# Second MoE of a fused attention and two-MoE kernel: its first product by seven products of blocks, and its loops with two blocks of tokens outermost

## The chip, the cores and the metric

The kernel runs on 1 core of a Trainium2 chip. Times are device microseconds (us) of that core for one execution; the runs of the kernel before have a median of 1211.6 us (3 runs, 1210.45 to 1211.93).

## What is computed

```python
attn = memory_attention(q, k, v, phi)          # 4 batches, 8 heads, 576 tokens, 64 wide
x = tokens_by_heads(attn)                      # 2304 x 512
h = x @ moe_w_in                               # first MoE, 2048 hidden
x = maximum(0.01 * h, h) @ moe_w_out
p = probs / (probs.sum(-1) + 1e-9)             # second MoE, 4 experts, 1024 hidden
for e in range(4):
    out += p[:, e:e + 1] * (maximum(x @ w1[e], 0) @ w2[e])
```

All of it is float32. A matmul here takes rounded operands (`float32r`), so every factor is split into a rounded high part and a rounded remainder, and every product is three matmuls: low x high, high x low, high x high.

## The kernel before

One list of operations, `Plan`, holds every step with an engine, a planned duration, a due time, and the tiles it reads and writes. `Plan.issue` walks a planned clock and, on each engine, issues the ready operation with the earliest due time; an operation with `also=` may go to a second engine. What comes out is a fixed order per engine, and the chip follows it, each instruction waiting for its semaphores. PSUM is eight banks, taken and given back through `Banks`.

Attention and the first MoE come first (up to about 409 us), then the second MoE. In its loops before, the expert is outermost, then the six blocks of TB = 384 tokens, then the eight chunks of 128 hidden units: 4 x 6 x 8 = 192 steps (`moe2_step`). A step is 12 matmuls of 384 columns for the first product (line 746: 4 pieces of the 512 inputs, 3 matmuls each), the rectifier on ScalarE (line 874, from PSUM, rounding to `hh`), the remainder on VectorE (line 876, from PSUM, to `hl`), and 9 matmuls of 512 columns for the second product (lines 889 to 891: 3 tiles of 128 tokens, 3 matmuls each). After eight chunks the three sums leave PSUM (line 899 on ScalarE for the first expert, line 901 on VectorE for the others). Tokens are split into parts again for each expert (`x_part`, through `split`, lines 224 and 227); weights are fetched once, into `raw` tiles by SP's queue, and split by `piece32`: the high part on ScalarE (line 224), the remainder on GpSimd or VectorE (line 227).

Of the kernel before, what the change touches and what calls it, by code (L numbers as in the profile page):

```python
# [19 lines left out]
class Banks:  # L20


    def __init__(self, psum, n):
        self.psum, self.n, self.at, self.uses = psum, n, None, 0
# [5 lines left out]
class Plan:  # L30
# [38 lines left out]
    def take(self, free, bank):  # L69

        if bank.at is not None:
            return True
        if bank.n == 2:
            at = [i for i in range(0, self.BANKS, 2) if {i, i + 1} <= free]
        else:
            at = sorted(free, key=lambda i: (i ^ 1) in free)
        if not at:
            return False
        bank.at = at[0]
        free.difference_update(range(at[0], at[0] + bank.n))  # L80
        return True

    def issue(self):
# [14 lines left out]
        while issued < len(ops):  # L98
            now = events[0][0]
            while events and events[0][0] <= now:  # L100
                _, n, what = heappop(events)
                if what is not None:
                    if isinstance(what, Banks):
                        banks.update(range(what.at, what.at + what.n))
                    continue
                for e, queue in zip(ops[n][0], (ready, spare)):
                    heappush(queue[e], (ops[n][1], n))
# [37 lines left out]
def kernel(  # L145
# [19 lines left out]
    P = 128  # L165
# [22 lines left out]
    AHEAD = 10.0  # L188
    MARGIN = 7.0
# [5 lines left out]
    const = ctx.enter_context(tc.tile_pool(name="const", bufs=1))  # L195
    wa = ctx.enter_context(tc.tile_pool(name="wa", bufs=1))
    beside = tc.tile_pool(name="m1", bufs=1, side="right")
    m1 = beside.__enter__()
# [5 lines left out]
    pr = const.tile([P, NTILE, E], F32, name="pr")  # L204
    raws = [const.tile([P, 1024], F32, name=f"raw{i}") for i in range(RAWS)]
    f64s = [const.tile([P, 512], F32, name=f"f64{i}") for i in range(F64S)]
    hh = [const.tile([P, TB], F32R, name=f"hh{i}") for i in range(NH)]
    hl = [const.tile([P, TB], F32R, name=f"hl{i}") for i in range(NH)]
    acc_all = const.tile([P, B - 1, KD, S], F32, name="acc")
    acc1 = [acc_all[:, b] for b in range(B - 1)]  # L210
    ah = [m1.tile([P, NGB, S], F32R, name=f"ah{b}") for b in range(B)]
    al = [m1.tile([P, NGB, S], F32R, name=f"al{b}") for b in range(B)]
    vt = m1.tile([P, B, HG, M], F32, name="vt")
    yh = [m1.tile([P, NGB, 2 * P], F32R, name=f"yh{i}") for i in range(NY)]
    yl = [m1.tile([P, NGB, 2 * P], F32R, name=f"yl{i}") for i in range(NY)]
    gt = [m1.tile([P, HB], F32, name=f"gt{i}") for i in range(NH)]
# [80 lines left out]

    cuts = [0] + UNITS1 + [NC1]
    units1 = [range(a, z) for a, z in zip(cuts, cuts[1:])]
    units2 = [range(NC1 + e * NC2, NC1 + (e + 1) * NC2) for e in range(E)]  # L300
# [9 lines left out]
    for u, unit in enumerate(units2):  # L310
        for j in range(NB):
            for i, c in enumerate(unit):
                steps.append((2, u, j, 0, c, u * NB + j, i == 0, i == len(unit) - 1))
# [5 lines left out]
    for i in range(n1, len(steps), NC2):  # L319
        for kk in range(KD):  # L320
            behind.setdefault(max(n1, i - NC2 + 2 + kk), []).append(("x", steps[i][5], kk))
    t = 0.0
    when = []
    for i, st in enumerate(steps):
# [4 lines left out]
        t += 3.95 if st[0] == 2 else 2.22 * (1.6 if st[1] == 0 else 1.0)  # L329
# [4 lines left out]
    attp = tc.tile_pool(name="attp", bufs=1)  # L334
    ap = attp.__enter__()
    ident = ap.tile([P, P], F32, name="ident")
# [3 lines left out]
    spare = acc_all.rearrange("p b k s -> p (b k s)")  # L340
    sizes = [HG * NC * M, HG * NC * D, 2 * HG * NC * D]
    alt = [spare[:, sum(sizes[:i]):sum(sizes[:i + 1])] for i in range(3)]
    pl = [ap.tile([P, HG, NC, M], F32, name="pl"), alt[0].rearrange("p (h c m) -> p h c m", h=HG, c=NC)]
    ql = [ap.tile([P, HG, NC, D], F32, name="ql"), alt[1].rearrange("p (h c d) -> p h c d", h=HG, c=NC)]
    kv = [
        ap.tile([P, 2, HG, NC, D], F32, name="kv"),
        alt[2].rearrange("p (i h c d) -> p i h c d", i=2, h=HG, c=NC),
    ]
    eT = ap.tile([P, NC * P], F32, name="eT")
    qT = ap.tile([P, 2, S], F32, name="qT")  # L350
    kb = ap.tile([P, 2, 2, M], F32, name="kb")
    pt = ap.tile([P, NC, HG, M], F32, name="pt")
    qt = ap.tile([P, NC, HG, D], F32, name="qt")
    a = ap.tile([P, NC, P], F32, name="a")
    k2 = ap.tile([P, 2, 2, D], F32, name="k2")
    NR = S // M
    at = [ap.tile([P, NR, M], F32, name=f"at{i}") for i in range(2)]
    aT = ap.tile([P, S], F32, name="aT")
    small = {
        nm: [ap.tile([P, n], F32, name=f"{nm}{i}") for i in range(2)]  # L360
        for nm, n in (("nmx", 1), ("z", 1), ("rz", 1), ("mx", NR), ("sm", NR))
# [222 lines left out]

    late = {}

    def att_done():
        attp.__exit__(None, None, None)
        accb = ctx.enter_context(tc.tile_pool(name="accb", bufs=1))
        acc1.append(accb.tile([P, KD, S], F32, name="acc3"))  # L590
        late["wb"] = ctx.enter_context(tc.tile_pool(name="wb", bufs=1))

# [3 lines left out]
    plan.op("X", 0.0, 0.0, att_done, [], everything + ["attention"])  # L596
# [7 lines left out]
    NA, RING = {"w1": 3, "w2": 6}, {"w1": 5, "w2": 10}  # L604
    got = {}

    def tiles(kind, n):
        if (kind, n) not in got:
            at = n % RING[kind]
            pool = wa if at < NA[kind] else late["wb"]  # L610
            shape = [P, KD, 2 * P] if kind == "w1" else [P, DM]
            if kind == "w1" and n < NP1:
                nm = f"w1h{at}"
                got[kind, n] = (pool.tile(shape, F32, tag=nm, name=nm),)
            else:
                got[kind, n] = [
                    pool.tile(shape, F32R, tag=f"{kind}{x}{at}", name=f"{kind}{x}{at}") for x in "hl"
                ]
        return got[kind, n]

# [16 lines left out]
    def piece32(kind, n, sl, src, due, key, after):  # L637
        raw, rk = raw_piece(src, due, after)

        size = 256 * src.shape[1] if kind == "w1" else DM  # L640
        split(due, size, lambda: tiles(kind, n)[0][sl], lambda: tiles(kind, n)[1][sl], lambda: raw, [rk],
              [key + "h", key + "l"])
# [39 lines left out]
    def pieces_of(kind, n):  # L682

        if kind == "w1" and n < NP1:
# [3 lines left out]
        elif kind == "w1":  # L688
            e, p = divmod(n - NP1, NP2)
            w1 = moe2_w1[e][:, 2 * P * p:2 * P * (p + 1)].rearrange("(k p) f -> p k f", p=P)  # L690
            yield partial(piece32, kind, n, (every, every), w1)
        elif n < NC1:
            yield partial(piece64, kind, n, (every, every), moe_w_out[n * P:(n + 1) * P, :])
        else:
            e, c = divmod(n - NC1, NC2)
            yield partial(piece32, kind, n, (every, every), moe2_w2[e][c * P:(c + 1) * P, :])

    wanted = {}
    for t, op in when:
        if op[0] == "y":  # L700
            wanted.setdefault(("w1", ys[op[1]][2]), t)
        elif op[0] == "s":
            if steps[op[1]][0] == 2:
                wanted.setdefault(("w1", steps[op[1]][4] // 2), t - AHEAD)
            wanted.setdefault(("w2", steps[op[1]][4]), t)
    parts = sorted((t, key) for key, t in wanted.items())
# [17 lines left out]
    def w_keys(kind, n):  # L724
        at = n % RING[kind]
        return [f"{kind}.{at}.{i}{x}" for i in range(2) for x in "hl"]

    def load_part(kind, n):
        at = n % RING[kind]
        after = ["attention"] if at >= NA[kind] else []  # L730
# [6 lines left out]
    freed = {"w1": 0, "w2": 0}  # L737
# [40 lines left out]
    def moe1_step(t, n):  # L778
# [22 lines left out]
        for d in range(KD):  # L801
# [10 lines left out]
            if last:  # L812
                key = ("acc", b, s, d)

                def fn(e="DVE", d=d, po=po):
                    a_ = acc1[b][:, d, s * HB:(s + 1) * HB]
# [4 lines left out]
                if u == 0:  # L821
                    after = ["attention"] if b == B - 1 else ["alt"]
# [5 lines left out]
    acc2, x2, pos = [], [], []  # L828

    def second():  # L830

        beside.__exit__(None, None, None)
        m2 = ctx.enter_context(tc.tile_pool(name="m2", bufs=1, side="right", reuse_waits="tile"))
        x2.extend([m2.tile([P, KD, TB], F32R, name=f"x{x}{i}") for x in "hl"] for i in range(2))
        acc2.extend(m2.tile([P, TPB, DM], F32, name=f"acc2{j}") for j in range(NB))

    def x_part(t, n, kk):

        x, j = n % 2, n % NB
        t -= AHEAD + 2.0  # L840
        at_ = j * TB
        while at_ < (j + 1) * TB:
            b, o = divmod(at_, S)
            m = min((j + 1) * TB - at_, S - o)
            xs = slice(at_ - j * TB, at_ - j * TB + m)

            def part(i, xs=xs):
                return x2[x][i][:, kk, xs]

            def src(b=b, o=o, m=m):  # L850
                return acc1[b][:, kk, o:o + m]
            split(t, m, partial(part, 0), partial(part, 1), src,
                  [("acc", b, s, kk) for s in range(2)] + ["second"], [f"xh{x}{kk}", f"xl{x}{kk}"])
            at_ += m

    def moe2_step(t, n):
        _, u, j, _, c, m, first, last = steps[n]
        h, x = n % NH, m % 2
        ph = Banks(psum, 1)
        cs = slice((c % 2) * P, (c % 2 + 1) * P)  # L860
# [99 lines left out]
```

## Time and profile before

| what | before |
|---|---|
| median of 3 runs | 1211.6 us |
| profiled execution, its own time | 1211.6 us |
| its span, first to last instruction | 1209.8 us |
| TensorE busy in the span | 98% |
| VectorE, ScalarE, GpSimd busy | 37%, 33%, 12% |
| mean granted TensorE clock, share of full | 0.993 |
| DMA, mean over the span | 46 GB/s |

A matmul's record overlaps the next one's, so what one costs is read from start to start. "Idle before" an instruction is time in which its engine stood still, with the engine and line that ended the wait.

### The profile page before, as it was taken

To read this page: it belongs to the slowest core of one execution; us is meant where nothing else is said; L and a number is where in the kernel's file an instruction comes from. 1 tells how busy PE (TensorE), PEld (TensorE's weight loads), DVE (VectorE), ACT (ScalarE), POOL (GpSimd) and SP (SyncE) were. 2 spreads that over 40 slices of the span, in tenths; PEclk is the share of its full clock that TensorE was granted. 3 is DMA by queue.
4 is the path that set the end of the run, shared out by engine and by line. 5 is a ranking of instruction groups with operands and counts; after the bars stand their busy time and mean duration, and the time that the engine had idled before them with its cause. 6 is when DMAs were issued, how large, how long until landed. Compare 5 with 4: busy or idle time off the path is not lost.

```text
span 1209.8 us, 17646 instructions
## 1 busy us (share of the span) xinstructions
PE 1181.5 (98%) x7408; PEld 1072.5 (89%) x7408; DVE 446.7 (37%) x817; ACT 397.5 (33%) x838; POOL 142.9 (12%) x108
## 2 busy tenths in 40 slices
PE   6799999999999999999999999999999999999998
PEld 4578999999999999999999999989999999999997
DVE  4977685932333412212322222252222232222211
ACT  4766774643343522212421111231111132111110
POOL 1522340410010300000320000130000030000000
PEclk9799999999999999999999999999999999999999
DMA  9754241300000300000210000030000020011011
GB/s 265 216 164 133 72 144 48 123 18 2 1 18 27 97 1 1 1 1 1 87 53 1 1 1 1 27 114 1 1 1 1 1 70 1 27 27 27 27 27 27
DMA packets 49071, 55.96 MB, mean 46 GB/s; under 512 B 11872, under 2 KB 36448, under 8 KB 48992
## 3 DMA queue, kind: packets, MB, share of 16 engines
q1 hardware_dynamic: 48992, 54.84, 15.5%
q8 instruction: 58, 0.95, 0.3%
q14 instruction: 21, 0.17, 0.0%
HBM read 50.11 MB, written 4.72 MB: 45 GB/s over the span
## 4 chain that ended last, share of the span: by engine, by line
PE 94%; DVE 3%; DMA 1%; issue 1%; ACT 1%; SPq 0%; POOL 0%; DVEq 0%; ACTq 0%
PE psum L746 41%; PE psum L890 11%; PE psum L891 11%; PE psum L889 11%; PE psum L808 6%; PE psum L810 5%; PE psum L809 5%; PE psum L761 2%; PE psum L448 1%; PE psum L465 1%; PE psum L514 1%; DMA ql<-in_q_dram 0%; DVE f L667 0%; DVE f L666 0%; DVE hl L227 0%
## 5 line engine op out<-in xcount | busy, mean ns | idle before, releaser
L876 DVE SCALAR_TENSOR_TENSOR hl<-psum,hh 128x384 fp32r<-128x384 f32 x192 | 107.1, 558 | 568.4 <-ACT hh L874 568.2
L874 ACT ACTIVATE hh<-psum 128x384 fp32r<-128x384 f32 x192 | 94.6, 493 | 592.8 <-PE psum L746 591.0
L746 PE MATMUL psum<-xh,w1h 128*128 128x384 f32 x768 | 258.4, 336 | 0.0
L746 PE MATMUL psum<-xl,w1h 128*128 128x384 f32 x768 | 257.3, 335 | 0.0
L890 PE MATMUL psum<-w2l,hh 128*128 128x512 f32 x576 | 225.2, 391 | 0.0
L891 PE MATMUL psum<-w2h,hh 128*128 128x512 f32 x576 | 224.8, 390 | 0.0
L889 PE MATMUL psum<-w2h,hl 128*128 128x512 f32 x576 | 224.4, 390 | 0.0
L746 PE MATMUL psum<-xh,w1l 128*128 128x384 f32 x768 | 164.8, 336 | 0.4 <-DVE hl L876 0.4
L808 PE MATMUL psum<-hh,w2l 128*128 128x288 f32 x512 | 154.8, 302 | 2.5 <-DVE acc L820 1.1
L746 PEld LDWEIGHTS psum<-xh,w1l 128*128 128x128 f32 x768 | 139.5, 188 | 15.5 <-DVE hl L876 0.8
L810 PE MATMUL psum<-hh,w2h 128*128 128x288 f32 x512 | 150.7, 294 | 0.0
L809 PE MATMUL psum<-hl,w2h 128*128 128x288 f32 x512 | 150.4, 294 | 0.0
L746 PEld LDWEIGHTS psum<-xh,w1h 128*128 128x128 f32 x768 | 144.3, 188 | 0.0
L746 PEld LDWEIGHTS psum<-xl,w1h 128*128 128x128 f32 x768 | 144.1, 188 | 0.0
L891 PEld LDWEIGHTS psum<-w2h,hh 128*128 128x128 f32 x576 | 108.1, 188 | 22.9
L889 PEld LDWEIGHTS psum<-w2h,hl 128*128 128x128 f32 x576 | 108.2, 188 | 16.1
L890 PEld LDWEIGHTS psum<-w2l,hh 128*128 128x128 f32 x576 | 108.2, 188 | 15.9
L227 DVE TENSOR_TENSOR hl<-gt,hh 128x288 fp32r<-128x288 f32 x127 | 69.7, 550 | 123.8 <-ACT hh L224 123.4
L808 PEld LDWEIGHTS psum<-hh,w2l 128*128 128x128 f32 x512 | 96.0, 188 | 12.8 <-issue 8.0
L227 POOL TENSOR_TENSOR w1l<-raw,w1h 128x1024 fp32r<-128x1024 f32 x14 | 33.7, 2406 | 612.1 <-ACT w1h L224 612.1
L810 PEld LDWEIGHTS psum<-hh,w2h 128*128 128x128 f32 x512 | 96.2, 188 | 0.0
L809 PEld LDWEIGHTS psum<-hl,w2h 128*128 128x128 f32 x512 | 96.2, 188 | 0.0
(100 smaller groups left out, 1178.7 us busy)
## 6 DMA issues: line engine op xcount, KB each, us to landing
raw<-in_moe_w_in_dram SPq DMA_DIRECT2D x16, 512.0 KB, 3.8
raw<-in_moe_w_out_dram SPq DMA_DIRECT2D x16, 512.0 KB, 3.5
raw<-in_moe_w_dram SPq DMA_DIRECT2D x16, 512.0 KB, 3.5
raw<-in_moe_w_dram SPq DMA_DIRECT2D x32, 256.0 KB, 2.7
kv<-in_v_dram SPq DMA_DIRECT2D x7, 512.0 KB, 5.4
ql<-in_q_dram SPq DMA_DIRECT2D x7, 512.0 KB, 6.1
kv<-in_k_dram SPq DMA_DIRECT2D x7, 512.0 KB, 4.7
out_dram<-acc SPq DMA_DIRECT2D x20, 128.0 KB, 2.4
```

What stands on the lines that cost most here:

```text
L227: engine(e).tensor_tensor(out=out, in0=in0, in1=in1, op=ALU.subtract)
L448: nc.tensor.transpose(pq[c * P:c * P + n], qt[0:n, c, 2 * j:2 * j + 2].rearrange("p h d -> p (h d)"), ident[0:n, 0:n],)
L746: nc.tensor.matmul(ps, lhsT=l, rhs=r, start=(n == 0), stop=(n == len(seq) - 1))
L761: nc.tensor.matmul(both()[hd * M:(hd + 1) * M, g, :], lhsT=vt[gs, b, hd, :], rhs=w1[gs, hd, :], start=True, stop=True,)
L808: nc.tensor.matmul(po, lhsT=w2l[:, ds_], rhs=th, start=first, stop=False)
L809: nc.tensor.matmul(po, lhsT=w2h[:, ds_], rhs=tl, start=False, stop=False)
L810: nc.tensor.matmul(po, lhsT=w2h[:, ds_], rhs=th, start=False, stop=last)
L874: plan.op("ACT", act(TB), e, lambda: nc.scalar.activation(out=th, in_=ph[0:TB], func=AF.Relu), [ph], [f"hh{h}"])
L876: plan.op("DVE", dve(TB), e, lambda: nc.vector.scalar_tensor_tensor(out=tl, in0=ph[0:TB], scalar=0.0, in1=th.bitcast(F32), op0=ALU.max, op ...
L889: nc.tensor.matmul(po, lhsT=tl[:, ts_], rhs=w2h, start=first, stop=False)
L890: nc.tensor.matmul(po, lhsT=th[:, ts_], rhs=w2l, start=False, stop=False)
L891: nc.tensor.matmul(po, lhsT=th[:, ts_], rhs=w2h, start=False, stop=last)
```

## The change

The first product of the second MoE goes over pairs: two blocks of 384 tokens, two chunks of hidden units, two halves of the inputs. These are 2 x 2 blocks, and an exact scheme gets the four sums from seven products of blocks instead of eight. Some factors are sums or differences of blocks: the tokens' are made in `x_parts`, once for each 768 tokens; the weights' in `piece_v1` (line 714). The seven products take turns in two PSUM banks (`share`); VectorE adds them up (line 988: one operand in PSUM, one in SBUF, result in SBUF), ScalarE rectifies (line 995), VectorE makes the remainder (line 997, both operands now in SBUF); the first product is copied out by ScalarE (line 1003). The second product does two chunks for six tiles of tokens, in the other six banks.

The loops are now: three blocks of 768 tokens outermost, then experts, then pairs of chunks: 3 x 4 x 4 = 48 units, each with 7 x 6 matmuls of 384 columns (line 980) and 6 x 6 of 512 (lines 1035 to 1037). Every weight of the second MoE is therefore fetched and split three times, in loads of 512 KB. Memory is laid out by hand in four large tiles (`exact`, `rounded`, `att` and later `late`, `w1`); the order names operands by these. The first MoE's sums lie in `xx`, and each 768 tokens' results replace them there.

```diff
+    units2 = [(j, e, p) for j in range(NB // 2) for e in range(E) for p in range(NP2)]
...
+    when.append((t, ("second",)))
+    for n, (j, e, p) in enumerate(units2):
+        if e == p == 0:
+            when.append((t - AHEAD2, ("x", j)))
+        when += [(t - AHEAD2, ("l1", n)), (t, ("l2", n))]
+        t += UNIT2
...
+    def piece_v1(kind, n, sl, src, due, key, after):
...
+        for out_, in0, in1, op, reads, key_ in (
+            (s1, a21, a22, ALU.add, [], "f640"), (s2, s1, a11, ALU.subtract, [], "f640"),
+            (s3, a11, a21, ALU.subtract, [], "f641"), (s4, a12, s2, ALU.subtract, ["f640"], "f641"),
+        ):
+            plan.op("DVE", 0.35, due, lambda e, o=out_, x=in0, y=in1, op=op: engine(e).tensor_tensor(
+                out=o, in0=x, in1=y, op=op), [rk, *reads], [key_], also=("POOL", 0.75))
+        srcs = (raw[:, :, 0:P], a22, f64s[0], f64s[1])
+        for i, (lo_, hi_) in enumerate(((0, 2), (2, 3), (3, 5), (5, 7))):
...
+            split(due, (hi_ - lo_) * 2 * P, partial(dst, 0), partial(dst, 1), lambda i=i: srcs[i],
...
+    def x_parts(t, j):
...
+        for k in range(2):
...
+            for i, in0, in1 in ((5, b12, b11), (1, b22, 5), (4, b21, 1), (3, b22, b12)):
...
+            for i in range(7):
+                split(t + i * 2.0 - 6.0, TB, lambda i=i, k=k: factors(i)[0][:, k], lambda i=i, k=k: factors(i)[1][:, k],
...
+    def first_products(t, n):
...
+        ps = [Banks(psum, 1, share) for _ in range(7)]
...
+                for i in range(2):
+                    seq += [(wl[:, slot, i], xh[:, i]), (wh[:, slot, i], xl[:, i]), (wh[:, slot, i], xh[:, i])]
+                for i, (l, r) in enumerate(seq):
+                    nc.tensor.matmul(ps[k][0:TB], lhsT=l, rhs=r, start=(i == 0), stop=(i == 5))
...
+        product(0)
+        p1, p1k, from_ = new_tmp()
+        plan.op("ACT", act(TB), at[0], lambda: nc.scalar.copy(p1, ps[0][0:TB]), [ps[0], from_], [p1k])
+        product(1)
+        u2 = add(1, p1, p1k)
+        product(2)
+        rectify(2, 0, 0, *add(2, p1, p1k))
+        product(3)
+        u3 = add(3, *u2)
+        product(4)
+        rectify(4, 1, 0, *add(4, *u3))
+        product(5)
+        u4 = add(5, *u2)
+        rectify(5, 1, 1, *add(5, *u3))
+        product(6)
+        rectify(6, 0, 1, *add(6, *u4))
...
-    def moe2_step(t, n):
...
+    def second_products(t, n):
...
+            plan.op("PE", 1.37, due, fn, [f"h{x}{k}" for x in "hl" for k in h] + w_keys("v2", n), [po])
```

What this makes of the order is read at two places. The first is TensorE in the middle of the second MoE. Before, a step's second product and the first product behind it (`x` are tokens' parts, `w1`, `w2` weights' parts, `h` the middle's, `h` and `l` high and remainder):

```order
L889 MATMUL psum<-w2h_4177,hl_78 128x512
L890 MATMUL psum<-w2l_4178,hh_74 128x512
L891 MATMUL psum<-w2h_4177,hh_74 128x512
L746 MATMUL psum<-xh_4186,w1l_2537 128x384 x4
L746 MATMUL psum<-xl_4187,w1h_2536 128x384
L746 MATMUL psum<-xh_4186,w1h_2536 128x384
```

Now, product 6 of one unit, products 0 and 1 of the next, and half of a second product:

```order
L1037 MATMUL psum<-late,rounded 128x512
L980 MATMUL psum<-rounded,w_3685 128x384 x6
L980 MATMUL psum<-late,rounded 128x384 x12
L1035 MATMUL psum<-late,rounded 128x512
L1036 MATMUL psum<-late,rounded 128x512
L1037 MATMUL psum<-late,rounded 128x512
```

First products of six matmuls now stand between second products of six, mostly one by one; once in two units three of them follow each other, as here, and at the next change of unit each has a second product behind it. With two banks for them, each needs the bank of the one before the last.

The second place is VectorE's queue. Before, remainders of the middle, and now and then the tokens':

```order
L876 SCALAR_TENSOR_TENSOR hl_76<-psum,hh_72 128x384
L876 SCALAR_TENSOR_TENSOR hl_77<-psum,hh_73 128x384
L876 SCALAR_TENSOR_TENSOR hl_78<-psum,hh_74 128x384
L876 SCALAR_TENSOR_TENSOR hl_79<-psum,hh_75 128x384
L227 TENSOR_TENSOR xl_4187<-acc,xh_4186 128x384 x4
```

Now, from the sum with product 6 of a unit to the sums with products 1, 2 and 3 of the next:

```order
L988 TENSOR_TENSOR exact<-psum,exact 128x384
L997 SCALAR_TENSOR_TENSOR rounded<-exact,rounded 128x384
L302 TENSOR_TENSOR rounded<-exact,rounded 128x256
L302 TENSOR_TENSOR rounded<-exact,rounded 128x512
L714 TENSOR_TENSOR exact<-exact 128x256 x2
L302 TENSOR_TENSOR late<-exact,late 128x512
L714 TENSOR_TENSOR exact<-exact 128x256 x2
L988 TENSOR_TENSOR exact<-psum,exact 128x384 x3
L997 SCALAR_TENSOR_TENSOR rounded<-exact,rounded 128x384
```

Between the two sums that give PSUM banks back stand one remainder of the middle, three remainders of weights (line 302) and the four sums of weights for a later unit (line 714). In all, the order puts 156 of the 240 remainders of 512 elements in the second MoE on GpSimd and 84 on VectorE. In the first half of the first MoE and in attention the order of all engines is the same as before.

## Rows read from the trace of the kernel before

**Rows 1.** The page's head, and its share of busy time for TensorE.
```profile
span 1209.8 us, 17646 instructions
PE 1181.5 (98%) x7408; PEld 1072.5 (89%) x7408; DVE 446.7 (37%) x817; ACT 397.5 (33%) x838; POOL 142.9 (12%) x108
```

**Rows 2.** Busy time by stretch: us, each engine's busy us (instructions), clock, DMA share, GB/s.
```profile
45.00:409.00 364.00, 358.68 (x3140) 330.98 (x3139) 207.43 (x384) 202.69 (x437) 82.83 (x60) 1.00 0.26 76
409.00:600.00 191.00, 191.00 (x977) 174.65 (x976) 45.08 (x86) 49.84 (x100) 12.93 (x8) 1.00 0.06 18
...
1000.00:1210.00 210.00, 203.93 (x1033) 185.20 (x1031) 52.16 (x98) 33.05 (x77) 1.29 (x1) 1.00 0.09 23
```

**Rows 3.** The chain that ended last, two first products: start, us, what.
```profile
413.83 2.08 PE psum L746 x12
...
769.30 2.08 PE psum L746 x12
```

**Rows 4.** Timeline, end of a first product: start, us, engine, line, operation [idle before].
```profile
1193.33 0.34 PE L746 MATMUL psum<-xh,w1h 128*128 128x384 f32 x1
1193.33 0.19 PEld L889 LDWEIGHTS psum<-w2h,hl 128*128 128x128 f32 x1
1193.50 0.39 PE L889 MATMUL psum<-w2h,hl 128*128 128x512 f32 x1
...
1193.70 0.49 ACT L874 ACTIVATE hh<-psum 128x384 fp32r<-128x384 f32 x1 [3.64 <-PE psum L746]
...
1194.23 0.56 DVE L876 SCALAR_TENSOR_TENSOR hl<-psum,hh 128x384 fp32r<-128x384 f32 x1 [3.58 <-ACT hh L874]
```

**Rows 5.** Groups by line and shape, VectorE: busy us, mean ns | idle before.
```profile
L227 DVE TENSOR_TENSOR hl<-gt,hh 128x288 fp32r<-128x288 f32 x127 | 69.7, 550 | 123.8 <-ACT hh L224 123.4
...
L667 DVE SCALAR_TENSOR_TENSOR f<-raw,f 128x512 uint32<-128x512 uint32 x32 | 26.7, 836 | 1.1
...
L666 DVE TENSOR_SCALAR f<-f 128x512 uint32<-128x512 uint32 x32 | 24.9, 778 | 1.1 <-ACT f L657 0.9
```

**Rows 6.** Timeline of VectorE, two runs of token remainders without a gap.
```profile
437.62 1.95 DVE L227 TENSOR_TENSOR xl<-acc,xh 128x384 fp32r<-128x384 f32 x4
...
602.96 1.96 DVE L227 TENSOR_TENSOR xl<-acc,xh 128x192 fp32r<-128x192 f32 x7
```

**Rows 7.** Timeline of GpSimd and VectorE, where both are at work.
```profile
606.53 2.43 POOL L227 TENSOR_TENSOR w1l<-raw,w1h 128x1024 fp32r<-128x1024 f32 x1 [0.37 <-ACT w1h L224]
606.63 2.55 DVE L227 TENSOR_TENSOR xl<-acc,xh 128x192 fp32r<-128x192 f32 x1
...
609.98 1.29 POOL L227 TENSOR_TENSOR w2l<-raw,w2h 128x512 fp32r<-128x512 f32 x1 [1.02 <-ACT w2h L224]
...
610.75 0.56 DVE L876 SCALAR_TENSOR_TENSOR hl<-psum,hh 128x384 fp32r<-128x384 f32 x1 [1.10 <-ACT hh L874]
```

**Rows 8.** VectorE by line: count, shortest/median/longest ns, first to last start.
```profile
L227 DVE TENSOR_TENSOR hl<-gt,hh x127: 395/459/1575, 46.9 to 404.3; 128x288 fp32r<-128x288 f32 x127
...
L666 DVE TENSOR_SCALAR f<-f x32: 362/421/1548, 29.7 to 234.7; 128x512 uint32<-128x512 uint32 x32
...
L667 DVE SCALAR_TENSOR_TENSOR f<-raw,f x32: 691/693/1868, 30.2 to 235.2; 128x512 uint32<-128x512 uint32 x32
...
L876 DVE SCALAR_TENSOR_TENSOR hl<-psum,hh x192: 544/557/559, 413.0 to 1198.4; 128x384 fp32r<-128x384 f32 x192
```

**Rows 9.** Timeline of TensorE: a wait in the second MoE.
```profile
798.64 0.97 PE L746 MATMUL psum<-xh,w1l 128*128 128x384 f32 x4 [0.40 <-DVE hl L876]
```

**Rows 10.** DMA issues from 405 us on: count, KB each, median us to landing.
```profile
raw<-in_moe_w_dram SPq DMA_DIRECT2D x11, 512.0 KB, 3.6
```

**Rows 11.** Timeline of the end: last sums out of PSUM, last outputs, last matmul.
```profile
1202.61 2.11 DVE L901 SCALAR_TENSOR_TENSOR acc<-psum,pr,acc 128x512 f32<-128x512 f32 x3 [3.69 <-PE psum L891]
...
1203.39 3.68 SPq L909 DMA_DIRECT2D out_dram<-acc  x6
1203.54 0.39 PE L891 MATMUL psum<-w2h,hh 128*128 128x512 f32 x1
```

More of the change, by code (lines that the diff above doesn't have):

```diff
@@ L76, in take @@
             at = sorted(free, key=lambda i: (i ^ 1) in free)
-        if not at:
+        if not at or bank.share == [0]:
             return False
+        if bank.share:
+            bank.share[0] -= 1
         bank.at = at[0]
@@ L212 @@
[L212 to L216, printed above, removed]
+    V1 = 7 * 2 * P
+    HALF = 2 * TB
+    SIZES = {"exact": 17104, "rounded": 22528, "att": 9168, "w1": 2 * V1}
+    whole = {nm: memory.tile([P, SIZES[nm]], F32R if nm == "rounded" else F32, tag=nm, name=nm) for nm in SIZES}
@@ new lines, with place, new @@
+    mark = dict.fromkeys((*SIZES, "late"), 0)
+    SIZES["late"] = SIZES["att"]
+    def place(nm, at, *shape):
+        n = 1
+        for size in shape:
+            n *= size
+        t = whole[nm][:, at:at + n]
+        if len(shape) > 1:
+            names = [f"d{i}" for i in range(len(shape))]
+            t = t.rearrange(f"p ({' '.join(names)}) -> p {' '.join(names)}", **dict(zip(names, shape)))
+        return t
+    def new(nm, n):
+        at = mark[nm]
+        mark[nm] += (n + 15) // 16 * 16 if n >= 16 else n
+        assert mark[nm] <= SIZES[nm], (nm, mark)
+        return at
@@ new lines, in exact @@
+    def exact(*shape):
+        n = 1
+        for size in shape:
+            n *= size
+        return place("exact", new("exact", n), *shape)
+    raws = [exact(1024) for _ in range(RAWS)]
+    f64s = [exact(512) for _ in range(F64S)]
+    pr = exact(NTILE, E)
+    xx = exact(KD, NT)
+    both_at = mark["exact"]
+    small_at = mark["exact"] = both_at + 2 * KD * 2 * P
+    vt = exact(B, HG, M)
+    gt = [exact(HB) for _ in range(NH)]
+    h_at = [new("rounded", HALF) for _ in range(NH)]
+    w2_at = [("rounded", new("rounded", 2 * DM)) for _ in range(6)] + [("late", new("late", 2 * DM)) for _ in range(4)]
@@ new lines @@
+    xc_at = [("late", new("late", HALF)) for _ in range(6)] + [("rounded", tok_at + i * HALF) for i in range(8)]
+    xc_from = ["attention", "tokens"]
+    v1_at = [("w1", 0)] + [("rounded", tok_at + 8 * HALF + i * 2 * V1) for i in range(2)]
+    assert v1_at[2][1] + 2 * V1 <= SIZES["rounded"]
+    v1_from = ["w_in", "hidden", "hidden"]
+    v2_at = [w2_at[6], w2_at[8], w2_at[0]]
+    v2_from = ["w_out6", "w_out8", "w_out0"]
+    tmp = [place("exact", both_at + i * TB, TB) for i in range(5)]
+    tmp += [place("exact", small_at + i * TB, TB) for i in range(4)]
@@ new lines, with renew, factors, tiles @@
+    tmp_from = ["w_in"] * 5 + ["hidden"] * 4
+    h_at += [w2_at[2][1] + i * HALF for i in range(NH)]
+    hh = [place("rounded", at, TB) for at in h_at]
+    hl = [place("rounded", at + TB, TB) for at in h_at]
+    h_from = [[]] * NH + [["w_out2"]] * NH
+    def renew(nm, was):
+        whole[nm] = memory.tile([P, SIZES[was]], F32R, tag=was, name=nm)
+    def factors(i):
+        return [place(*xc_at[2 * i + x], 2, TB) for x in range(2)]
+    def tiles(kind, n):
+        if kind == "w1":
+            return (place(*w1_at[n % 5], KD, 2 * P),)
+        nm, at = {"w2": w2_at, "v1": v1_at, "v2": v2_at}[kind][n % RING[kind]]
+        shape = {"w2": (DM,), "v1": (7, 2, P), "v2": (2, DM)}[kind]
+        n = {"w2": DM, "v1": V1, "v2": 2 * DM}[kind]
+        return [place(nm, at + x * n, *shape) for x in range(2)]
@@ L351 @@
[L351 to L355, printed above, removed]
+    eT = tile_([NC * P])
+    qT = exact(2, S)
+    kb = tile_([2, 2, M])
+    pt = exact(NC, HG, M)
+    qt = tile_([NC, HG, D])
+    a = tile_([NC, P])
+    k2 = exact(2, 2, D)
     NR = S // M
[L357 removed]
@@ L826, in moe1_step @@
         freed["w2"] += b == B - 1 and s == 1
[L828 to L854, printed above, removed]
```

303 lines of the change are left out of this document (167 added, 136 removed).

## The prediction

> **What bounds the kernel now.** I read the busy shares first, then the table by stretch, then the chain that ended last, then single pieces of the timeline. TensorE is busy 98% of the span and no other engine reaches 40% [rows 1]. By stretch it loses 5.3 us between 45 and 409 us and nothing that shows in the first 191 us of the second MoE [rows 2]. In the chain the second MoE is a train of first products: from 413.83 to 769.30 us there are 86 steps, 4.133 us each, and of each step 2.08 us is the first product's 12 matmuls [rows 3]. So a matmul of 384 columns costs 0.1733 us from start to start and one of 512 (4.133 - 2.08)/9 = 0.228 us; the pair in the timeline shows 0.17 between two starts [rows 4]. The clock is at its full level, 2.4 GHz, in these stretches [rows 2]. The longest wait of a matmul inside this stage is 0.40 us [rows 9]. The stage is matmuls in a row, so a matmul less is its whole cost less, as long as nothing new makes TensorE wait.
>
> The profiled execution took 1211.6 us, which is also the median of the runs; its span is 1209.8 [rows 1], with 1.8 us around it. Changes under 0.2% (2.4 us) can't be told from none.
>
> **What is removed.** Before, 192 steps of 12 matmuls for the first product; now 48 units of 42. That is 2304 - 2016 = 288 matmuls less, by 0.1733 = **49.9 us**. The second product keeps its 1728 matmuls. A unit is 42 x 0.1733 + 36 x 0.228 = 15.5 us of TensorE, where four steps were 16.5.
>
> **What is added on TensorE's side: nothing. Beside it, three things.**
>
> DMA: weights are fetched three times, two loads of 512 KB per unit where the landing of one takes 3.6 us [rows 10]. Two in 15.5 us, fetched into three tiles, leave SP's queue over half its time; taken at 0.
>
> ScalarE: per unit one copy, four rectifiers, some six roundings of weights and one of tokens; 12 instructions near 0.5 us [rows 4] are 6 us of 15.5; 0, except as a link in VectorE's waits.
>
> VectorE is the one to reckon. Four instructions of 384 in a row take 1.95 us, so 0.47 each; seven of 192 take 1.96, so 0.28 each [rows 6]; between them 256 is 0.34, and 512 about 0.62. Per unit: seven sums from PSUM 3.3, four remainders of the middle 1.9, four sums of weights 1.4, 1.75 remainders of 512 and one of 256 1.4, a 48th of the tokens' 66 instructions 0.6, sums leaving PSUM 54/48 x 0.68 (three in 2.11 us, overlap off [rows 11]) 0.8. Together 9.4 us of 15.5, where four steps took 3.9 (45.08 us of VectorE in 191 us [rows 2]). It fits, but VectorE's order now stands between TensorE and its two banks.
>
> **The lock between VectorE and GpSimd.** The timeline shows a VectorE instruction of 192 elements, 0.28 us by itself, that starts 0.1 us after a GpSimd instruction and ends 0.22 us behind it, 2.55 us long; four microseconds later a VectorE instruction that reads PSUM runs 0.56 us inside a GpSimd instruction, untouched [rows 7]. The groups say the same: instructions that work from SBUF alone reach 1.5 to 1.9 us, the 192 that read PSUM stay within 544 to 559 ns [rows 8]. What it costs on average: in the first MoE, mean less median is 91 ns x 127 + 357 x 32 + 143 x 32 = 27.6 us [rows 5, 8], for some 60 GpSimd instructions [rows 2], so 0.46 us for each.
>
> The Trainium skill (SBUF — State Buffer, section "SBUF: two separate sides") states this as a rule: VectorE and GpSimd share a port pair, locked for a whole instruction, and a VectorE instruction with two SBUF inputs loses it to a GpSimd instruction that began first. The trace agrees with it, with the 2.55 us above. The rule speaks against this change, which moves the middle's remainder (line 997) from a PSUM to an SBUF operand and puts 156 more remainders on GpSimd; with every GpSimd instruction in VectorE's way in full, it gives the second rival below.
>
> From rows: GpSimd has 156/48 = 3.25 instructions of about 1.3 us [rows 7] per unit; at 0.46 that is 1.5 us more for VectorE, at most 3.25 x 1.3 = 4.2. Where it hits: VectorE's order between the sum with product 6 and that with product 1 of the next unit. After TensorE ends product 6: 0.2 until the sum starts, 0.47 for it, 0.53 for ScalarE [rows 4], 0.47, then 0.34 + 0.62 + 0.62 + 4 x 0.34 of weights' work: free at 4.6 us. At this change of unit product 1 ends two second products and two first ones later, 2 x 1.37 + 2 x 1.04 = 4.8 us, and its sum may start at 5.0. Product 3, which needs that bank, stands 2.4 us behind product 1's end; the sum and the signal take 0.7 of it. So VectorE may lose 5.0 - 4.6 + 1.5, about 1.9 us here before TensorE stands still. Three GpSimd instructions fall here: 1.4 us on average, 3.9 at worst. At the other change of unit, where three products follow each other, only one remainder stands before the sum, and there the spare is about 1.8 us. The stop is thus between 0 and 2 us per two units; I take 0.4, near the low end because the average just fits: 24 x 0.4 = **10 us**, bounds 0 and 48.
>
> **Change of tokens.** Twice, the next 768 tokens' factors (8 differences and 14 remainders, 22 x 0.47 = 10.3 us of VectorE) must be made while the last unit with the old ones runs: two units' VectorE work, 2 x 8.8 + 10.3 + 3 of lock, is 31 us, as much as the two units' TensorE time. 0 to 5 us each, I take 2: **4 us**. At the start of the second MoE the same work lies beside the first MoE's last steps, and seven products are issued with few second products between them; 0 to 8, I take **3 us**.
>
> **End.** Before, the last three sums leave PSUM in a row, until 1.2 us after the last matmul starts, and six outputs queue up for 3.7 us [rows 11]. Now tiles end 1.37 us apart, one output pair behind each: **-1 us**, bounds -2 and +1.
>
> **Sum.** 1211.6 - 49.9 + 10 + 4 + 3 - 1 = 1177.7, so 1178 us.
>
> **Rivals.** *The cover holds.* Every sum finds its slack, TensorE never waits: 1211.6 - 49.9 - 1 = 1161, with some start-up up to 1167. For it: the trace's 40% of VectorE still unused, and that only one wait of 0.40 us shows where weights were split before. Chance 0.2.
>
> *GpSimd's instructions stand in VectorE's way nearly in full.* 1.5 us per two units, 36, with 5 at each change of tokens and 8 at the start: 1211.6 - 49.9 + 36 + 10 + 8 - 1 = 1215 at the very worst; half of the waits in full gives 1190 to 1205. For it: remainders on both engines become ready at the same moment, when a unit's buffers come free. Against it: the 0.46 us measured. Chance 0.2.
>
> *VectorE sets the pace, slower than before.* Its time per unit passes TensorE's old 16.5 us: 9.4 + 4.2 for the lock in full + four times 0.75 us of standing still until ScalarE has rectified = 16.6. Then 48 x 16.6 = 797 us in place of 794, and with starts and changes of tokens about 1225. It needs all three at once, and much of the standing still lies in time when VectorE has nothing to do. Chance 0.07.
>
> *The saving is smaller than the count says.* The new order of matmuls (weights' remainder, high, high, by halves) might not keep 0.1733 us; at 0.19, the record of a weight load [rows 4], 2016 x 0.017 = 34 us would go, and the forecast's sum would be 1212. Against it: before, the same loads stand in front of matmuls 0.17 us apart, so they overlap [rows 4]. Chance 0.03.
>
> **Numbers.** Forecast 0.5 (1167 to 1190), rivals 0.2, 0.2, 0.07, 0.03. The range 1163 to 1200 leaves out the slower rival, the upper part of the second and the low edge of the first. Faster by over 0.2% (below 1209): the first three cases, 0.90; within: the last, 0.03; slower: 0.07.
>
> **What would show it.** Right: L980 starts 0.173 us apart within a product; TensorE's idle time in the second MoE near 15 us, in pieces under 2 us, put down to the sums of line 988; VectorE's lines 302, 714 and 997 with longest records near 2 us and line 988 without; VectorE busy near 70% there. Wrong: waits put down to a DMA or to ScalarE's roundings, starts further apart than 0.173 inside products, one long stop at 409 us, or the period of two units at 31.0 us throughout.

## The result: slower by 1.2%, and the profile after

The changed kernel takes 1225.9 us (median of 4 runs, 1225.3 to 1227.3) against 1211.3 for the kernel before on the same chip: 1.0123 times as long, interval 1.0105 to 1.014. The prediction, 1178 us and a range of 1163 to 1200, missed, and on the wrong side. The profiled execution took 1227.3 us, its span is 1225.5.

From its page: the busy shares, the granted clock in 40 slices, the chain by engine, and two groups of VectorE (busy us, mean ns, idle time before and who ended it).

```profile
span 1225.5 us, 18258 instructions
PE 1158.5 (95%) x7120; PEld 1028.2 (84%) x7120; DVE 811.6 (66%) x1405; ACT 505.6 (41%) x1040; POOL 297.5 (24%) x226
PEclk9799999999999999999999899999999899999999
...
PE 75%; DVE 18%; issue 3%; ACT 2%; DMA 0%; SPq 0%; POOL 0%; DVEq 0%; ACTq 0%
...
L988 DVE TENSOR_TENSOR exact<-psum,exact 128x384 f32<-128x384 f32 x336 | 181.5, 552 | 149.1 <-PE psum L980 148.1
L714 DVE TENSOR_TENSOR exact<-exact 128x256 f32<-128x256 f32 x192 | 106.7, 574 | 2.7
```

TensorE's instructions fell by 288, from 7408 [rows 1] to 7120, as counted. But its busy share fell from 98 to 95%, and 18% of the chain that ended last is VectorE. VectorE is not out of time: it is 66% busy, and before the sums of line 988 it stood 149 us still, waiting for TensorE's products. The two engines wait for each other in turn. The clock shows 0.8 in two slices past the start.

Whom TensorE waited for in the second MoE (us in total, times, longest):

```profile
PE psum L980 <- DVE exact L988: 34.9, 27, 2.6
PE psum L980 <- DVE exact L1048: 3.0, 2, 1.5
PE psum L1035 <- ACT exact L1003: 1.3, 1, 1.3
```

And by stretch (us, then each engine's busy us, clock, DMA share, GB/s): the start, three stretches within a block of tokens, and between them the two changes of tokens.

```profile
409.00:450.00 41.00, 36.88 (x191) 32.55 (x190) 36.68 (x62) 16.34 (x33) 18.41 (x13) 1.00 0.28 90
450.00:650.00 200.00, 193.72 (x957) 171.21 (x956) 136.56 (x232) 70.01 (x140) 51.97 (x38) 1.00 0.20 64
650.00:710.00 60.00, 51.61 (x229) 45.00 (x228) 47.46 (x77) 21.89 (x45) 17.39 (x12) 0.91 0.27 79
710.00:930.00 220.00, 212.75 (x1050) 187.82 (x1048) 152.60 (x256) 79.53 (x160) 60.97 (x44) 1.00 0.21 65
930.00:990.00 60.00, 52.54 (x234) 46.23 (x235) 46.19 (x78) 21.98 (x45) 16.13 (x12) 0.91 0.28 79
990.00:1150.00 160.00, 154.70 (x764) 136.56 (x762) 106.92 (x182) 56.15 (x112) 40.15 (x31) 1.00 0.19 63
```

Idle time of TensorE is the length less the first busy number: 4.1 us at the start, 6.3, 7.3 and 5.3 us in the regular stretches, 8.4 and 7.5 us at the changes of tokens, 38.8 us together. At the changes the granted clock also falls to 0.91: a part of those 60 us ran at 1.2 GHz in place of 2.4. By this mean about 5 us of full speed are lost at each (0.09 x 60), 10 us together. Before, TensorE lost nothing in the stretch from 409 to 600 us [rows 2].

One regular stop in detail (start, us, engine, line; in brackets the wait):

```profile
521.28 1.29 POOL L302 TENSOR_TENSOR w<-exact,w 128x512 fp32r<-128x512 f32 x1 [1.52 <-ACT w L299]
...
521.44 2.96 DVE L714 TENSOR_TENSOR exact<-exact 128x256 f32<-128x256 f32 x2
...
522.37 1.21 PE L980 MATMUL psum<-late,rounded 128*128 128x384 f32 x6
...
522.83 1.29 POOL L302 TENSOR_TENSOR rounded<-exact,rounded 128x512 fp32r<-128x512 f32 x1 [0.26 <-ACT rounded L299]
...
524.32 0.68 DVE L302 TENSOR_TENSOR rounded<-exact,rounded 128x512 fp32r<-128x512 f32 x1
...
524.92 0.75 DVE L714 TENSOR_TENSOR exact<-exact 128x256 f32<-128x256 f32 x2
525.59 0.54 DVE L988 TENSOR_TENSOR exact<-psum,exact 128x384 f32<-128x384 f32 x1
...
526.19 1.31 PE L980 MATMUL psum<-late,rounded 128*128 128x384 f32 x6 [1.23 <-DVE exact L988]
```

Two sums of weights (line 714), which a little later take 0.75 us, take 2.96 us here. The line merges the two; one by one in the trace, the first takes 1.41 us and ends 0.3 us behind the first of two remainders on GpSimd, the second takes 1.51 us and ends 0.3 us behind the other. The sum that TensorE needs comes 2.2 us later for it, and TensorE stands still for 1.23 us. It is what [rows 7] showed, at the place that the prediction named.

### The profile page after: what moved, and what is told of

It reads as the page before. It is cut to its first block, busy times and chain, and to the rows that moved or that the text cites. A ratio compares the mean times of both kernels' runs of the same rounds, so it can differ in the third digit from the quotient of the medians.

```text
span 1225.5 us, 18258 instructions
## 1 busy us (share of the span) xinstructions
PE 1158.5 (95%) x7120; PEld 1028.2 (84%) x7120; DVE 811.6 (66%) x1405; ACT 505.6 (41%) x1040; POOL 297.5 (24%) x226
## 4 chain that ended last, share of the span: by engine, by line
PE 75%; DVE 18%; issue 3%; ACT 2%; DMA 0%; SPq 0%; POOL 0%; DVEq 0%; ACTq 0%
PE psum L980 23%; PE psum L833 8%; PE psum L1037 8%; PE psum L1036 8%; PE psum L1035 8%; PE psum L895 5%; PE psum L897 5%; PE psum L896 5%; DVE exact L714 4%; DVE rounded L302 3%; DVE exact L988 3%; DVE rounded L997 2%; PE psum L848 2%; DVE late L302 1%; DVE exact L1048 1%
## 5 line engine op out<-in xcount | busy, mean ns | idle before, releaser
L988 DVE TENSOR_TENSOR exact<-psum,exact 128x384 f32<-128x384 f32 x336 | 181.5, 552 | 149.1 <-PE psum L980 148.1
L302 DVE TENSOR_TENSOR rounded<-exact,rounded 128x288 fp32r<-128x288 f32 (+3 forms) x228 | 159.4, 710 | 122.8 <-ACT rounded L299 119.9
L302 POOL TENSOR_TENSOR rounded<-exact,rounded 128x512 fp32r<-128x512 f32 (+1 forms) x96 | 135.3, 1412 | 332.8 <-ACT rounded L299 228.4
L299 ACT CAST rounded<-exact 128x512 fp32r<-128x512 f32 (+2 forms) x322 | 157.0, 515 | 27.3 <-DVE exact L302 10.6
L980 PE MATMUL psum<-rounded 128*128 128x384 f32 x768 | 158.6, 342 | 8.9 <-DVE exact L988 8.9
L997 DVE SCALAR_TENSOR_TENSOR rounded<-exact,rounded 128x384 fp32r<-128x384 f32 x192 | 111.5, 581 | 69.5 <-ACT rounded L995 69.2
L980 PEld LDWEIGHTS psum<-rounded 128*128 128x128 f32 x768 | 138.1, 191 | 21.7 <-DVE exact L988 14.9
L1037 PE MATMUL psum<-late,rounded 128*128 128x512 f32 x384 | 152.9, 398 | 0.0
L1036 PE MATMUL psum<-late,rounded 128*128 128x512 f32 x384 | 152.4, 397 | 0.0
L1035 PE MATMUL psum<-late,rounded 128*128 128x512 f32 x384 | 151.0, 393 | 1.3 <-ACT exact L1003 1.3
L980 PE MATMUL psum<-late,rounded 128*128 128x384 f32 x576 | 116.4, 341 | 16.6 <-DVE exact L988 13.6
L833 PE MATMUL psum<-rounded 128*128 128x288 f32 x768 | 125.0, 299 | 3.3 <-DVE att L604 1.7
L895 PE MATMUL psum<-rounded 128*128 128x288 f32 x384 | 116.4, 303 | 2.6 <-DVE exact L907 1.1
L833 PEld LDWEIGHTS psum<-rounded 128*128 128x128 f32 x768 | 109.4, 190 | 7.7 <-issue 2.7
L897 PE MATMUL psum<-rounded 128*128 128x288 f32 x384 | 112.9, 294 | 0.0
L896 PE MATMUL psum<-rounded 128*128 128x288 f32 x384 | 112.9, 294 | 0.0
L714 DVE TENSOR_TENSOR exact<-exact 128x256 f32<-128x256 f32 x192 | 106.7, 574 | 2.7
```

Of the source, the lines that this page charges most:

```text
L299: nc.scalar.copy(out, in_) if e == "ACT" else engine(e).tensor_copy(out, in_)
L302: engine(e).tensor_tensor(out=out, in0=in0, in1=in1, op=ALU.subtract)
L714: plan.op("DVE", 0.35, due, lambda e, o=out_, x=in0, y=in1, op=op: engine(e).tensor_tensor(out=o, in0=x, in1=y, op=op), [rk, *reads], [key ...
L833: nc.tensor.matmul(ps, lhsT=l, rhs=r, start=(n == 0), stop=(n == len(seq) - 1))
L895: nc.tensor.matmul(po, lhsT=w2l[:, ds_], rhs=th, start=first, stop=False)
L896: nc.tensor.matmul(po, lhsT=w2h[:, ds_], rhs=tl, start=False, stop=False)
```

## The experiments

Theory A: the lock between VectorE and GpSimd delays the sums. Rival B: VectorE's amount and order of work does. Rival C: clock and spacing. Theory D came later, from the bank numbers. The versions that leave work out or add useless work, and the one with eight products, were run once each, the others 4 or 10 times.

**All remainders of the second MoE on VectorE.** In `split`, for the second MoE:

```diff
+            if alone:
+                plan.op("DVE", dve(n), due, lambda: subtract("DVE", lo(), src(), hi().bitcast(F32)),
+                        (*reads, keys[0]), [keys[1]])
+                return
```

> All remainders of the second MoE on VectorE, GpSimd has none there; the same results. Theory A (the lock between VectorE and GpSimd holds up the sums that free the two banks): the regular stops and most of those at the changes of tokens go, though VectorE gets some 2 us more work per unit: 1180 to 1192 us. Rival B (VectorE's amount and order of work holds up the sums): more work on VectorE, so 1226 or slower, up to 1245. Rival C (clock and matmul spacing explain most): 1215 to 1226.

Measured: 1168.8 us (1168.1 to 1169.4), 0.9656 of the kernel before (0.964 to 0.9672). That is 57 us less than the changed kernel, and faster than both. Its busy shares, TensorE's only listed wait in the second MoE, and one stretch:

```profile
PE 1140.2 (98%) x7120; PEld 1022.1 (88%) x7120; DVE 801.2 (69%) x1561; ACT 507.2 (43%) x1040; POOL 78.2 (7%) x70
...
PE psum L984 <- DVE exact L992: 0.8, 2, 0.4
...
450.00:1150.00 700.00, 699.23 (x3479) 625.45 (x3478) 511.51 (x1006) 261.61 (x524) 0.00 (x0) 1.00 0.21 68
```

VectorE does 156 remainders more and is less long busy than in the changed kernel, 801 us against 812. B is out as it stands: more work on VectorE, and TensorE waits 0.8 us in all. The time lies below the range of A, too: the gain is larger than A expected. C is out as the main cause: the second product's matmuls stand 0.231 us apart in both kernels, and the clock's 10 us went with the stops.

**GpSimd's remainders left out, order kept.**

```diff
+                    lambda e: None if e in skip else subtract(e, lo(), src(), hi().bitcast(F32)),
...
+        skip=("POOL",) if n >= 3 else ()
```

> From the fourth unit on, GpSimd's remainders of the weights are left out (TensorE takes the remainders of the first three units); every other instruction stays in its place, VectorE's queue among them. Theory A: VectorE's instructions that work from SBUF alone fall back to their own 0.41 to 0.62 us, the regular stops go: 1183 to 1195. Rival B: VectorE has the same work in the same order, so the stops stay: 1218 to 1226.

Measured: 1175.2 us. VectorE has the same 1405 instructions in the same order, and is busy for 83 us less (the page's shares; TensorE's longest list of waits in the second MoE; the sums of weights as a group):

```profile
PE 1140.0 (97%) x7120; PEld 1021.1 (87%) x7120; DVE 728.3 (62%) x1405; ACT 506.5 (43%) x1040; POOL 95.5 (8%) x82
...
PE psum L981 <- DVE exact L989: 3.4, 4, 1.6
...
L715 DVE TENSOR_TENSOR exact<-exact 128x256 f32<-128x256 f32 x192 | 81.4, 443 | 2.7
```

The mean of a weights' sum is 443 ns, where the page of the changed kernel has 574. A stands: the same work in the same order takes VectorE less time, and of 34.9 us of waits for its sums 3.4 are left, most of them in the first units, where GpSimd still works. The time is again below the range of A.

**The sums of weights left out, order kept** (`n < 3 and engine(e).tensor_tensor(...)` at line 714).

> From the fourth unit on the four sums of weights (line 714) are left out (their tiles keep what the first units put there); order otherwise the same. Theory A: half of the instructions that GpSimd can hold up are gone, the others stay: about half the stops go, 1195 to 1208. Rival B: 2.2 us of 17 us of VectorE's time per unit go, and the whole surplus with it: 1175 to 1190.

Measured: 1187.8 us, 38 us less than with them. That lies in B's range and not in A's. The half that A expected was too little: the sums of weights are only 25 of the 83 us that the run above gave back to VectorE (106.7 - 81.4), but they stand right ahead of the sums that free the banks. This run takes away both the delay and the work, so it can't tell A from B; B fails in the two runs before. That their place makes them count for more is argued here, not shown.

**Tokens' factors made once** (in `x_parts`, nothing is issued for `j > 0`).

> The factors of the second and third 768 tokens are not made: the products there use the first tokens' factors; order otherwise the same. If the two changes of tokens cost 13 to 14 us each, half clock included, as read from the trace: 1197 to 1203. If what is lost there is only moved from the units around it: 1212 or more.

Measured: 1206.6 us, 19 us less, with the clock at 0.993 in place of 0.983 on average. It falls between the two ranges: the two changes of tokens cost some 10 us each, about half of it by the clock, and of the 13 to 14 that I had read a part only moves.

**Useless work on GpSimd**, added to the version with all remainders on VectorE, first subtractions, then copies:

```diff
+                if n == 512 and keys[0].startswith("v1"):
+                    plan.op("POOL", pool(n), due, lambda: nc.gpsimd.tensor_tensor(
+                        out=idle, in0=hi().bitcast(F32), in1=idle, op=ALU.subtract), [keys[0]], [])
```

> The version with all remainders on VectorE, plus three subtractions of 512 on GpSimd per unit (144 in all) whose result nobody uses; each starts when a weight's high part is there. Theory A (the lock alone): the stops come back though nothing waits for GpSimd's results: 1205 to 1240. Rival B (what was lost before came from work that waited for GpSimd's remainders, or from buffers it held): 1167 to 1172, as without them.

Measured: 1256.0 us, above the range. The busy shares, TensorE's longest list of waits, and GpSimd's useless instructions:

```profile
PE 1163.3 (93%) x7120; PEld 1023.7 (82%) x7120; DVE 913.7 (73%) x1561; ACT 506.7 (40%) x1040; POOL 287.5 (23%) x215
...
PE psum L989 <- DVE exact L997: 52.0, 51, 3.2
...
L319 POOL TENSOR_TENSOR idle<-rounded,idle 128x512 f32<-128x512 f32 x96 | 140.7, 1465 | 417.1 <-ACT rounded L301 414.4
```

> As the run with useless subtractions, but GpSimd copies (one input) in place of subtracting (two inputs). If every GpSimd instruction that works in SBUF holds VectorE up for its whole length: 1190 to 1240, by the copies' length. If only its instructions with two inputs do: 1167 to 1173.

Measured: 1180.0 us, below the first range and above the second:

```profile
PE 1146.3 (97%) x7120; PEld 1020.5 (87%) x7120; DVE 833.3 (71%) x1561; ACT 507.0 (43%) x1040; POOL 189.8 (16%) x215
...
L319 POOL COPY idle<-rounded 128x512 f32<-128x512 f32 x96 | 74.9, 780 | 432.5 <-ACT rounded L301 430.6
```

Nothing reads what these 144 instructions write (one more fills the tile at the start), and VectorE's own instructions take 112.5 us longer for them: the stops are back. So it is the engines' use of SBUF at the same time that costs, not a wait for data. Copies do it too, for less. Three pairs of runs, by the differences of their pages and times:

| GpSimd's work in the second MoE | instructions | VectorE busy longer | for each | run longer |
|---|---|---|---|---|
| useless copies | 144 | 32.1 us | 0.22 us | 11.2 us |
| the change's remainders (against the run with the same order) | 144 | 83.3 us | 0.58 us | 50.7 us |
| useless subtractions | 144 | 112.5 us | 0.78 us | 87.2 us |

The pairs' kernels differ, so this is rough, but the time grows faster than VectorE's: of the first 32 us 11 reach the end, of the next 51 us 40, and for the last 29 the run is 36 us longer. A part of that is the clock, 0.983 and 0.987 on average in the longer runs of the last two pairs, 0.992 or 0.993 in the other runs of the table.

**Eight plain products in the new loops**, no sums of tokens or weights, all remainders on VectorE (`first_products` with four sums of 12 matmuls, each rectified from PSUM):

> The new loops and memory with eight plain products of blocks (four sums of 12 matmuls per unit, rectified straight from PSUM), no sums of tokens or weights, all remainders on VectorE. Against the version with seven products it has 288 matmuls of 384 columns more, 0.1733 to 0.175 us each, and no sums for TensorE to wait for: 1212 to 1222. If the new loops by themselves cost more than the wider matmul spacing: above 1225. If the scheme saves less than its count says: below 1205.

Measured: 1215.6 us, 4.6 above the kernel before, and 46.8 above the version with seven products. The scheme's saving is there.

**The kernel before, remainders on VectorE** (the same `alone`, for its weights and tokens):

> The kernel before, with the second MoE's remainders of weights and tokens on VectorE alone. If the lock costs time only where TensorE waits for VectorE's next instruction: no difference, 1208 to 1213. If GpSimd's remainders cost the kernel before too: 1195 to 1205.

Measured: 1210.2 us, 0.9995 of the kernel before (0.9985 to 1.0004). The lock was there (VectorE's remainders of weights took 1.66 us, shown below, and take 0.69 in this run) and cost nothing that shows. Two things are different from the changed kernel, and this run doesn't part them: TensorE hardly waited for VectorE, 0.40 us at most [rows 9], and the second MoE had 38 GpSimd instructions in place of 156.

**Tiles of the second product in pairs.**

> The version with all remainders on VectorE, the second product's tiles taken in pairs: three matmuls into one bank, three into the other, and again, as before the change, where never more than three in a row went to one bank. If six matmuls in a row into one bank are what widened the spacing from 0.228 to 0.231 us: back to 0.228 and 4 to 6 us faster, 1163 to 1166. If the spacing has another cause (the operands' places, the mix of products): 0.231 as before, 1167 to 1172.

Measured: 1174.4 us (1173.0 to 1174.6), slower than without. From start to start the second product's matmuls take 0.230 us on average between 450 and 1150 us, 0.231 without, 0.228 in the kernel before. So six matmuls in a row into one bank are at most a third of it; the rest is open. And TensorE stands still for 3.9 us of these 700 us, where it was 0.8, so the new order makes it wait.

**Remainders on VectorE in the first MoE too** (`alone=True` by default).

> The version with all remainders on VectorE, now in attention and the first MoE too (GpSimd keeps only the sums of 64-bit halves there). If the lock costs time only where TensorE waits for VectorE: at most the 5 us that TensorE loses between 45 and 409 us, and VectorE's added work may cost as much: 1164 to 1171. If freeing VectorE of the lock is a gain everywhere: below 1164.

Measured: 1166.5 us (1166.1 to 1167.0), 0.9637 (0.9622 to 0.9651), inside the first range, and the fastest version.

**Banks in turn.** The stop shown above can't be understood from the lock alone: the product at 526.19 waits for the sum with the product directly before it, though the product before that had left its bank long ago. `take` (line 77) prefers a free bank whose neighbour is taken, and of two such the lower number; so a product often gets the bank that was just given back. Counted in the planned order, 136 of 335 products take the bank of the product directly ahead of them (101 of them with one second product between the two); in this stretch five in a row have one bank, from the product at 515.05 to the one at 526.19.

```diff
-            at = sorted(free, key=lambda i: (i ^ 1) in free)
+            at = sorted(free, key=(lambda i: self.taken.get(i, 0)) if bank.share else (lambda i: (i ^ 1) in free))
...
+        self.turn += 1
+        self.taken[bank.at] = self.turn
```

> The changed kernel with one thing different: a first product takes the bank that has been free longest. Every engine's order stays the same, GpSimd's remainders too; only bank numbers move. In the changed kernel 136 of the 335 products that follow another took the very bank of the product before them, so their start waits for a sum that is one product old, not two. Theory D (half of what TensorE loses comes from these): 1200 to 1215. Theory A alone (VectorE is late by more than either distance allows): 1222 to 1227, no change.

Measured: 1194.3 us (1193.6 to 1194.4), 0.9861 of the kernel before (0.9846 to 0.9876): 31.6 us less and more than D expected, with the order of every engine and all of GpSimd's work as they were. The same burst in its timeline:

```profile
518.16 2.96 DVE L717 TENSOR_TENSOR exact<-exact 128x256 f32<-128x256 f32 x2
...
519.55 1.29 POOL L305 TENSOR_TENSOR rounded<-exact,rounded 128x512 fp32r<-128x512 f32 x1 [0.26 <-ACT rounded L302]
...
521.04 0.68 DVE L305 TENSOR_TENSOR rounded<-exact,rounded 128x512 fp32r<-128x512 f32 x1
...
521.52 1.21 PE L983 MATMUL psum<-late,rounded 128*128 128x384 f32 x6
521.65 0.75 DVE L717 TENSOR_TENSOR exact<-exact 128x256 f32<-128x256 f32 x2
...
522.32 1.01 DVE L991 TENSOR_TENSOR exact<-psum,exact 128x384 f32<-128x384 f32 x2
...
522.92 1.33 PE L983 MATMUL psum<-rounded 128*128 128x384 f32 x6 [0.18 <-DVE exact L991]
```

The pair of sums takes 2.96 us again. But the product at 521.52, the one that had to stand still, goes on without a stop, and the next one waits 0.18 us. By stretch:

```profile
409.00:450.00 41.00, 36.97 (x192) 33.12 (x191) 36.27 (x61) 16.02 (x32) 17.60 (x13) 1.00 0.28 90
450.00:650.00 200.00, 199.01 (x984) 176.68 (x982) 142.25 (x238) 74.70 (x150) 57.11 (x41) 1.00 0.20 66
650.00:710.00 60.00, 54.16 (x263) 47.08 (x264) 50.68 (x87) 22.54 (x46) 16.54 (x12) 1.00 0.30 88
710.00:930.00 220.00, 216.44 (x1071) 192.45 (x1069) 160.92 (x270) 84.58 (x171) 61.26 (x44) 1.00 0.20 64
930.00:990.00 60.00, 56.97 (x278) 49.58 (x277) 44.62 (x76) 19.40 (x40) 16.25 (x13) 1.00 0.30 91
990.00:1150.00 160.00, 159.64 (x795) 142.60 (x793) 113.19 (x189) 58.47 (x118) 44.03 (x32) 1.00 0.19 60
```

TensorE's idle time is 4.0 us at the start, 1.0, 3.6 and 0.4 in the regular stretches, 5.8 and 3.0 at the changes: 17.8 us where there were 38.8, and the clock stays at 1.00.

> All remainders on VectorE, in the first MoE too, and the first products' banks in turn. TensorE loses only 0.8 us to sums with all remainders on VectorE, so Theory A and Theory D both say no change against that version's 1166.5: 1164 to 1168. A gain of more than 2 us would say that waits too short to be listed as such were lost in the spacing.

Measured: 1167.4 us (1166.3 to 1168.3), no change, as expected. Banks in turn alone take 32 of the 57 us, GpSimd's absence alone takes all of them and leaves nothing for the other. The loss thus needed both: late sums, and products that wait for the sum just before them.

## Why the prediction was wrong

**The saving was right.** 288 matmuls at 0.1733 us were to give 49.9 us; seven products against eight, both without the lock, differ by 46.8.

**The step that failed is the spare of 1.9 us, and with it the 10 us for TensorE's stops.** The prediction had each product wait for the bank of the product before the last ("Product 3, which needs that bank, stands 2.4 us behind product 1's end"), and the chapter on the change says so too. It was inferred from the number of banks, and is untrue for 136 of 335. For 101 of those the slack between a product's end and the next product's start is one second product, 1.37 us, and the sum and its signal take 0.7 of it. (By the step's own numbers the spare was 5.0 - 4.6 and 2.4 - 0.7, so 2.1; that slip is not what failed.) With GpSimd out of the way the kernel is 57 us faster, where the terms for the lock, the changes and the start added up to 17. With the banks in turn, which is what was reckoned with, TensorE's idle time from 409 to 1150 us is 17.8 us in place of 38.8, and the kernel 31.6 us faster.

Idle time understates the stops, for a matmul's record still runs for some 0.17 us when the next one could start [rows 4]. Counted from start to start in the trace (after 409 us, at the full clock, every start that comes more than a quarter late), TensorE loses 49 us in the changed kernel, 26 with the banks in turn and 2 with all remainders on VectorE. With 7.7 us for the spacing, worked out below, the sum then closes: 1211.6 - 49.9 - 1 + 7.7 + 26 = 1194 with the banks in turn, where 1194.3 was measured; and with 49 in place of 26, and 10 for the clock, 1227 for the changed kernel, whose profiled execution took 1227.3. So even with the banks in turn the 17 us were 9 too few: the start shows 4.0 us of idle time for a term of 3, the two changes 8.9 for 4.

**The lock itself was sized nearly right, and used wrongly.** 0.46 us for each GpSimd instruction was forecast, 0.58 measured. Line 997, singled out for its new operand, bears little of it: 111.5 us of busy time against 107.6 in the run with the same order and no GpSimd. (The "156 more remainders" on GpSimd are all of them; before there were 38. The sum uses 156 rightly.) But "near the low end because the average just fits" took a mean where both engines start from one event: a load lands, ScalarE rounds, and GpSimd's remainders and VectorE's sums of the same weights become ready together, right ahead of the sums that free banks. A row of before showed how this looks, and I had not read it: VectorE's remainders of weights in the second MoE (groups of VectorE, 405 to 1210 us):

```profile
L227 DVE TENSOR_TENSOR w2l<-raw,w2h 128x512 fp32r<-128x512 f32 x9 | 14.9, 1657 | 12.7 <-ACT w2h L224 12.7
```

1.66 us each, where the same subtraction takes 0.69 without GpSimd. The Trainium skill (SBUF — State Buffer, section "SBUF: two separate sides") calls the shared pair an exclusive lock for the whole instruction; the trace agrees, with the two sums of weights, 0.41 us alone, that took 1.41 and 1.51 us, each until just behind a GpSimd instruction.

**"What is added on TensorE's side: nothing" was off by 7.7 us.** The spacing of the matmuls grew, for the second product from 0.228 to 0.231 us. Six units apart, the same first product in the version with all remainders on VectorE:

```profile
450.18 1.21 PE L984 MATMUL psum<-late,w 128*128 128x384 f32 x6
...
544.16 1.21 PE L984 MATMUL psum<-late,w 128*128 128x384 f32 x6
```

93.98 us for six units is 15.66 each, with next to no wait, where 15.5 was reckoned: 48 x 0.16 = 7.7 us, and 1211.6 - 49.9 - 1 + 7.7 = 1168.4; that version takes 1168.8. In the changed kernel six units take 98.11:

```profile
457.17 1.21 PE L980 MATMUL psum<-late,w 128*128 128x384 f32 x6
...
555.28 1.21 PE L980 MATMUL psum<-late,w 128*128 128x384 f32 x6
```

16.35 each, just under the 16.5 of four steps before. So between the changes of tokens the saving was nearly eaten, and the changes and the start turned it into a loss.

**The changes of tokens** were put at 2 us each. They cost about 10 each, some 5 of it by the clock, which no term had.

**The signs.** Right: waits put down to line 988; line 988 untouched at 552 ns on average, line 714 stretched; VectorE busy for 70% of the time from 450 to 1150 us (by the table) for "near 70%"; DMA and ScalarE in nobody's way but for one wait of 1.3 us. Wrong in size: 38.8 us of idle time by stretch for "near 15", and pieces of up to 2.6 us for "under 2".

**The rivals.** The one that ends slower gave "about 1225", and the time is 1225.9; still its mechanism isn't this. It had VectorE set the pace, at more than 16.5 us per unit; VectorE stood still for 149 us before the sums, and more work on it (all remainders) made the kernel faster. The nearest was GpSimd's instructions in VectorE's way in full, whose "very worst" was 1215, still on the assumption that banks take turns.

## What to carry to other kernels

Two buffers are two only if the allocator hands them out in turn: read the bank numbers of consecutive products before reckoning slack with them. Price a contended port at the burst where both engines become ready from the same event, with the row of the instruction that runs there, not with a mean over a stage. Work given to GpSimd beside a VectorE on which TensorE waits may cost more than it takes off: here 156 remainders moved back to VectorE made it less busy, and the kernel 57 us faster.

## What the runs showed of the hardware that was not expected

GpSimd copies, with one input, hold VectorE up as well: 144 of them, 0.76 to 0.78 us on average, cost VectorE 32 us. The lock works both ways: in the trace a useless subtraction that starts while VectorE is at work from SBUF alone takes 1.52 us on average, any other 1.30; a useless copy 0.88 and 0.62. With stops of up to 2.6 us at the changes of tokens the granted clock fell to 0.91 over 60 us; with the same work and shorter stops, banks in turn, it stayed at 1.00. And the second product's matmuls stand a little further apart in the new loops for a reason that the runs left open.
